# Weight forms made once for two groups, sums that read PSUM directly, and sigmoid products and projection sums at other places in the queues

## The chip, the cores and the metric

The kernel runs on one core of a Trainium2 chip. The metric is the device time of one execution in microseconds (us); of several executions the median is given. TensorE (PE) multiplies matrices and writes into PSUM, its weight load (PEld) overlaps its matmuls; VectorE (DVE), ScalarE (ACT) and GpSimd (POOL) do element-wise work, SyncE (SP) issues transfers. Each engine works off its own queue in order, and waits on semaphores for the others.

## The reference, cut to what matters

```python
# r, k, v: (4, 8, 768, 48); w, u: (8, 48)
for t in range(S):
    cur = einsum('bhd,bhe->bhde', u[None] * kt, vt)
    y[:, :, t] = einsum('bhd,bhde->bhe', rt, state + cur)
    state = w[None, :, :, None] * state + einsum('bhd,bhe->bhde', kt, vt)
x = y.transpose(0, 2, 1, 3).reshape(3072, 384)
g = x @ w_gate                       # (384, 1536)
silu = g * (1.0 / (1.0 + exp(-g)))
val = x @ w_val                      # (384, 1536)
out = silu * val @ w_out             # (1536, 384)
```

A linear attention with decay runs over 768 positions, and its output passes through a gated feed-forward block. All of it is fp32. This change concerns the feed-forward block alone.

## The kernel before, in words

The 3072 tokens are cut into 24 blocks of 128 (6 chunks of positions by 4 batches), and two blocks make a group, so there are 12 groups. The attention is computed block by block in a loop over s; between its steps, pieces of the feed-forward block that are ready are taken from a list `todo` (`feed`, `gaps`). Everything is issued in an order that the Python code writes out: `manual_schedule` keeps each engine's queue in that order, and the framework adds semaphores and gives tiles their buffers.

Groups 0 and 1 compute gate and value by plain products (`gate_value`, L445). Groups 2 to 7 go in pairs through `four_units` (L638): 7 products and 4 more in place of 12 for each block of 128 columns of the weights. Groups 8 to 11 go in two pairs, called group 8 and group 10 here, through `three_units` (L788). It takes three blocks of 128 columns (f = 3t to 3t+2) by three blocks of the 384 inputs by the two groups of tokens, and makes the result of 18 block products from 15 (`ROUNDS`, L672). A unit t (0 to 3) has 15 steps; each step (`three_step`, L774) multiplies a weight form by a token form, for gate and for value (o = 0, 1). Seven chains of steps accumulate in PSUM banks: n, y, l4, l5, l1, l2 and l8, of which n, y, l5, l1 and l8 share four buffers of pool ps_a.

- `in_place(t)` (L689) turns three of the nine weight blocks of unit t into forms where they lie in `wgv`, with six operations on GpSimd. It is called in `prepare_threes` (L760) at projection items 0, 2, 4 and 6 of groups 6 and 7, after `four_units` is through with these weights.
- `w_forms(g, t)` (L701) makes the six other forms r2, r3, r13, r11, r5 and r9, with nine operations on GpSimd (L720), in a ring buffer or in `spare`, a list of tiles that the attention no longer needs. It is done once for group 8 and once more for group 10: for group 8 and t = 0 at projection item 7, for group 10 and t = 0, 1 at items 2 and 6 of group 8's projections, for the others during unit t - 1, one operation behind each of its steps.
- `x_forms(g)` (L730) makes eleven sums of token blocks on VectorE (L744 to L754).
- `later(at, do, out, ...)` (L800) puts an operation behind step `at` of the unit, in the queue of its engine; z = 15 t. A name in quotes is a PSUM bank. ScalarE copies banks into SBUF tiles (q10, q14, r12, r6, x, y), VectorE adds up the six results c[0] to c[5], and GpSimd adds y to r6 (L827).
- `silu` (L803) issues a sigmoid on ScalarE (L806) and two products (L807, L808) on the engine `on`, behind step `muls`. For c[4], c[5] these are on GpSimd; for the other results of units 0 to 2 they are on VectorE, both pairs behind step 7 of the next unit; in unit 3 one pair is on VectorE and one on GpSimd.
- `two_projections(g)` (L652) multiplies the hidden values by w_out in seven products per group in place of eight (`project`, L499), in the order of 14 items "00 10 01 02 11 04 03 12 05 06 13 14 15 16" (first digit: which of the two groups). Their input sums come from `h_sums` (L487, operations at L493, L494, L496 and L497), in a ring buffer hs of pool `three`, tag w_bits, with three buffers.

At the end (L1033 to L1042) the list `tail` puts the units of group 8, its projections, the units of group 10 (whose first two steps stand among the last projections) and its projections in one order.

```python
later(z + 10.4, dve.tensor_add, c[2], y, "l1")
later(z + 10.5, dve.tensor_add, c[5], q10, "l5")
later(z + 11.5, dve.tensor_add, r12, r12, "l2")
later(z + 12.5, dve.tensor_add, c[3], r6, "l8")
```

Step 13 adds to bank l1 again, step 14 to l2; so step 13 waits until c[2] has been read from l1, and step 14 until r12 has read l2 (in unit 3 these two steps change places).

Of the kernel before, what the change touches and what calls it, by code (L numbers as in the profile page):

```python
# [9 lines left out]
FP32 = mybir.dt.float32  # L10
# [12 lines left out]
def fast(  # L23
# [47 lines left out]
    wcol = cst.tile([P, HP], FP32, name="wcol")  # L71
    ub = cst.tile([P, H, D], FP32, name="ub")
    kscale = cst.tile([P, H, D], FP32, name="kscale")
    rscale = cst.tile([P, H, D], FP32, name="rscale")
    w128 = cst.tile([P, HP], FP32, name="w128")
# [150 lines left out]
    def own_product(i):  # L226
        kl, rl = raw(i)
        rk = two.tile([P, H, D], FP32, name="rk", tag="rk")[:]
        pool.tensor_mul(rk, rl, kl)
        pool.tensor_mul(rk, rk, ub[:])  # L230
        rks[i] = rk
# [16 lines left out]
    sp.dma_start(  # L248
        out=ub[:].rearrange("p h d -> p (h d)"),
        in_=bass.AP(tensor=u.tensor, offset=u.offset, ap=[[0, P], [1, H * D]]),  # L250
# [50 lines left out]
    def scale_k(i):  # L301
        pool.tensor_mul(khat[i % 4][:, :, 0:D], raw(i)[0], kscale[:])

    def scale_r(i):
        pool.tensor_mul(rhat_of(i)[:, :, 0:D], raw(i)[1], rscale[:])  # L305

    def natural_tables():
        for t, dst in ((pw[:, :, 1 : P + 1], kscale), (pv, rscale)):
            t_ps = ps_a.tile([P, HP, P], FP32, name="t_ps", tag="a")
            for a in range(HP):  # L310
                pe.transpose(t_ps[:, a, :], t[:, a, :], ident[:])
            act.copy(dst[:], t_ps[:].rearrange("p a (e x) -> p (a e) x", e=2)[:, :, 0:D])

# [173 lines left out]
    def h_sums(g, n):  # L487
        h11, h12, h21, h22 = h_quarters(g)
        t = three.tile([P, 2, FH, P], FP32, name="hs", tag="w_bits")
        x = part_of.setdefault(g, {})  # L490
        x["s"] = x.get("s", ()) + (t[:, 0], t[:, 1])
        if n == 0:
            dve.tensor_add(t[:, 0], h22, h21)  # L493
            dve.tensor_sub(t[:, 1], t[:, 0], h11)  # L494
# [143 lines left out]
    def four_units(g):  # L638

        steps = sorted((11 * f - 5 + at, f, what) for f in range(FC) for what, at in PLACE.items())  # L640
        pieces = [[] for _ in range(26)]
        n = 0
        for at, f, what in steps:
            k = max(n - 1, 0) if n < 4 else 3 + min(23 * (n - 4) // (11 * FC - 4), 22)
            if what == "p1" and f % 2 == 0 and f + 2 < FC:
                pieces[k].append(lambda f=f: w_sums(g, f + 2))
            k = (0, 1, 2, 2)[n] if n < 4 else k
            pieces[k].append(lambda f=f, what=what: four(g, f, what))
            n += what[0] in "pc"
        return [lambda q=q: [do() for do in q] for q in pieces]  # L650

    def two_projections(g):  # L652

        def item(j, p):
            if (j, p) in ((1, 0), (0, 1)):
                h_sums(g, p)
# [29 lines left out]
    spare += [t[:].rearrange("p a x -> p (a x)")[:, 0:256] for t in v_ld + Z]  # L686
    wide = {}

# [11 lines left out]

    def w_forms(g, t):  # L701

        f = 3 * t
        made = wide["u", g, t] = {}

        w = [[wgv[:, :, c, P * (f + i) : P * (f + i + 1)] for c in range(CC)] for i in range(3)]
        def place():
            if g > THREES and t < 2:
                s = [x.rearrange("p (o t) -> p o t", o=2) for x in spare[6 * t : 6 * t + 6]]
            else:  # L710
                ring = three.tile([P, 6, 2, P], FP32, name="s", tag="w_bits")
                s = [ring[:, n] for n in range(6)]
            made.update(zip(("r2", "r3", "r13", "r11", "r5", "r9"), s))
            made.update({
                "r0": w[1][1], "r1": w[0][1], "r4": w[0][0], "r6": w[1][2], "r7": w[2][2],
                "r8": w[1][0], "r10": w[2][0], "r12": w[0][2], "r14": w[2][1],
            })

        return [place] + [
            lambda o=o, a=a, b=b, op=op: op(made[o], made[a], made[b])  # L720
            for o, a, b, op in (
                ("r2", "r14", "r6", pool.tensor_sub), ("r3", "r8", "r1", pool.tensor_sub),
# [37 lines left out]
    def prepare_threes(g, n):  # L760
        if g == THREES:
            if n in (0, 2, 4, 6):
                in_place(n // 2)
            if n == 7:
                for do in w_forms(g, 0):
                    do()
        else:
            if n == 10:
                x_forms(g)
            if n in (2, 6):  # L770
                for do in w_forms(g, n // 4):
                    do()

    def three_step(g, t, n):  # L774
# [6 lines left out]
        u, v = wide["u", g, t][what], wide["v", g][what]  # L781
        for o in range(2):
# [5 lines left out]
    def three_units(g):  # L788
# [14 lines left out]
        def silu(at, n, which, h, on, muls):  # L803
# [4 lines left out]
            todo.append((muls + 0.1, lambda: on.tensor_mul(h, sg, value)))  # L808

        for t in range(4):  # L810
            z = 15 * t
            for n in range(15):
                todo.append((z + n, lambda t=t, n=n: three_step(g, t, n)))
            if ("u", g, t + 1) not in wide and t < 3:
                forms = w_forms(g, t + 1)
                todo.append((z + 0.1, forms[0]))
                todo += [(z + n + 0.2, do) for n, do in enumerate(forms[1:])]
            later(z + 0.5, act.copy, q10, "n")
# [6 lines left out]
            later(z + 8.5, act.copy, x, "n")  # L825
            later(z + 9.5, act.copy, y, "y")
            later(z + 9.6, pool.tensor_add, r6, y, r6)  # L827
            later(z + 10.4, dve.tensor_add, c[2], y, "l1")
            later(z + 10.5, dve.tensor_add, c[5], q10, "l5")
            later(z + 11.5, dve.tensor_add, r12, r12, "l2")  # L830
# [14 lines left out]
        pieces = []  # L845
# [188 lines left out]
    projections = two_projections(THREES), two_projections(THREES + 2)  # L1034
    for t in range(2):
        wide["u", THREES + 2, t] = None
    threes = three_units(THREES), three_units(THREES + 2)
# [418 lines left out]
```

## Time and profile before

| what | before |
| --- | --- |
| median of 3 runs | 629.29 us (628.3 to 630.57) |
| the profiled execution | 627.92 us, of it 626.2 us from the first to the last instruction (the span) |
| TensorE clock granted | 0.997 |
| TensorE busy | 604.1 us |
| VectorE / GpSimd / ScalarE busy | 404.1 / 374.3 / 234.7 us |
| units of group 8 | 449.4 to 506.4 us |
| projections of group 8 | 506.4 to 537.6 us |
| units of group 10, from step 2 | 537.6 to 591.3 us |
| projections of group 10, output | 591.3 to 626.2 us |

All times within the execution are us from its first instruction. A line of the timeline gives start, duration, engine, line of the code, operation, output and inputs with their shapes, how many instructions follow each other, and in brackets how long the engine had been idle before it, and for which instruction it waited. In the table of waits a line gives who waited for whom, the total in us, how many times, and the longest one.

### The profile page before, as it was taken

How to read it: one execution, taken by the hardware profiler on the slowest of the kernel's cores; microseconds unless marked ns; L12 is line 12 of the kernel's file. 1: busy time of each engine (PE TensorE's matmuls, PEld its weight loads, DVE VectorE, ACT ScalarE, POOL GpSimd, SP SyncE). 2: the span in 40 equal slices, each digit the busy share in tenths (PEclk: the TensorE clock that was granted, in tenths of full speed). 3: DMA queues.
4: the chain of work that ended last, by engine and by line, in shares of the span. 5: the costliest groups of instructions: out<-in, count | busy, mean ns of one | idle time of the engine just before them, and what ended most of it. 6: DMA issues, size and time to landing. Idle time of an engine off the chain costs nothing.

```text
span 626.2 us, 12872 instructions
## 1 busy us (share of the span) xinstructions
PE 604.1 (96%) x4992; PEld 541.6 (86%) x4992; DVE 404.1 (65%) x737; ACT 234.7 (37%) x599; POOL 374.3 (60%) x414
## 2 busy tenths in 40 slices
PE   8799999999999999999999999999999989999986
PEld 7688888899888899888899888899887779977886
DVE  6878997373556573466575466666457896588770
ACT  3368785312444412344331334532233320233310
POOL 4789789935566315475453647389857459178210
PEclk9999999999999999999999999999999999999998
DMA  7989873234232113323222311230100000000001
GB/s 178 228 213 250 258 240 65 49 63 85 55 59 35 38 18 72 69 40 55 37 40 62 76 20 29 33 49 17 39 1 2 1 1 26 26 0 1 1 2 54
DMA packets 138006, 40.45 MB, mean 65 GB/s; under 512 B 128592, under 2 KB 131792, under 8 KB 137936
## 3 DMA queue, kind: packets, MB, share of 16 engines
q1 hardware_dynamic: 134480, 34.82, 26.2%
q10 hardware_dynamic: 3456, 4.72, 2.1%
q8 instruction: 41, 0.67, 0.5%
q14 instruction: 29, 0.24, 0.1%
HBM read 28.51 MB, written 4.72 MB: 53 GB/s over the span
## 4 chain that ended last, share of the span: by engine, by line
PE 76%; DVE 10%; POOL 4%; issue 1%; SPq 1%; DMA 1%; ACT 1%; DVEq 0%; ACTq 0%; POOLq 0%
PE c_b L620 13%; PE o_f L520 12%; PE c_a L620 11%; PE o_a L520 7%; PE gv L449 7%; PE c_l L783 6%; PE o_b L520 6%; PE y_ps L412 5%; PE s_ps L382 3%; DVE hats L801 3%; PE c_n L783 2%; DVE hTs L808 2%; PE c_y L783 2%; DVE At L807 2%; SPq L359 1%
## 5 line engine op out<-in xcount | busy, mean ns | idle before, releaser
L449 PE MATMUL gv<-xT,wgv 128*128 128x256 f32 x288 | 66.8, 385 | 0.6 <-ACT xT L416 0.6
L323 ACT ACTIVATE At<-ident,du 128x128 f32<-128x128 f32 x176 | 61.0, 396 | 16.2 <-DVE du L235 7.3
L620 PE MATMUL c_b<-xT,wgv 128*128 128x256 f32 x216 | 64.5, 380 | 0.0
L604 POOL TENSOR_TENSOR hTs<-hTs,u 128x256 f32<-128x256 f32 x36 | 28.7, 799 | 56.4 <-DVE hTs L603 56.2
L449 PEld LDWEIGHTS gv<-xT,wgv 128*128 128x128 f32 x288 | 53.2, 190 | 8.9 <-ACT xT L416 0.9
L620 PEld LDWEIGHTS c_b<-xT,wgv 128*128 128x128 f32 x216 | 40.7, 190 | 5.3
L387 DVE COPY_PREDICATED At<-mask,s_ps 128x512 f32<-128x512 int32 x48 | 33.0, 743 | 18.0 <-PE s_ps L382 9.4
L627 ACT COPY u<-c_a 128x256 f32<-128x256 f32 x72 | 26.7, 371 | 47.0 <-PE c_a L620 46.0
L620 PE MATMUL c_a<-t,s 128*128 128x256 f32 x144 | 43.5, 383 | 0.4 <-ACT p L627 0.4
L620 PE MATMUL c_a<-xT,wgv 128*128 128x256 f32 x144 | 42.8, 379 | 0.0
L305 POOL TENSOR_TENSOR hats<-r_ld,rscale 128x384 f32<-128x384 f32 x20 | 21.1, 1057 | 33.8 <-DMA hats<-hats 33.8
L600 ACT ACTIVATE sg<-hTs 128x256 f32<-128x256 f32 x72 | 29.9, 416 | 30.2 <-DVE hTs L629 21.3
L620 PE MATMUL c_b<-xT,s 128*128 128x256 f32 x144 | 37.0, 379 | 0.0
L634 DVE TENSOR_TENSOR u<-u,c_b 128x256 f32<-128x256 f32 x36 | 15.0, 417 | 33.0 <-PE c_b L620 30.1
L412 PE MATMUL y_ps<-At,v_ld 128*32 128x128 f32 x768 | 34.9, 273 | 1.4 <-DVE At L387 1.4
L801 POOL TENSOR_TENSOR kT<-y,kT 128x512 f32<-128x512 f32 x8 | 11.5, 1440 | 38.0 <-ACT y L801 38.0
L412 PEld LDWEIGHTS y_ps<-At,v_ld 128*32 128x32 f32 x768 | 30.3, 110 | 2.4 <-issue 1.4
L582 POOL TENSOR_TENSOR s<-wgv 128x256 f32<-128x256 f32 x18 | 13.3, 738 | 30.6 <-PE o_f L520 28.8
L440 POOL TENSOR_TENSOR Z<-Z,w 48x192 f32<-48x192 f32 x32 | 18.1, 567 | 21.7 <-DVE Z L439 20.5
L620 PEld LDWEIGHTS c_a<-t,s 128*128 128x128 f32 x144 | 26.8, 190 | 4.4 <-ACT p L627 0.8
L620 PEld LDWEIGHTS c_b<-xT,s 128*128 128x128 f32 x144 | 27.2, 190 | 3.9
L620 PEld LDWEIGHTS c_a<-xT,wgv 128*128 128x128 f32 x144 | 27.3, 190 | 3.6
(217 smaller groups left out, 1600.0 us busy)
## 6 DMA issues: line engine op xcount, KB each, us to landing
hats<-hats SPq DMA_DIRECT2D x192, 32.0 KB, 2.0
w_bits<-in_moe_w_gate_dram SPq DMA_DIRECT2D x6, 768.0 KB, 5.9
v_ld<-in_v_dram SPq DMA_DIRECT2D x48, 96.0 KB, 3.3
w_bits<-in_moe_w_val_dram SPq DMA_DIRECT2D x6, 768.0 KB, 6.3
w_bits<-in_moe_w_out_dram SPq DMA_DIRECT2D x6, 768.0 KB, 6.5
out_dram<-o_sb ACTq DMA_DIRECT2D x24, 192.0 KB, 2.0
k_ld<-in_k_dram SPq DMA_DIRECT2D x20, 192.0 KB, 3.0
r_ld<-in_r_dram SPq DMA_DIRECT2D x20, 192.0 KB, 3.8
```

The source lines that it names most:

```text
L305: pool.tensor_mul(rhat_of(i)[:, :, 0:D], raw(i)[1], rscale[:])
L323: lambda h=h: act.activation(At[i % 2][:, h, :], ident[:], AF.Identity, scale=du[:, h : h + 1])
L387: dve.copy_predicated(At[i % 2][:].rearrange("p (a e) t -> p a e t", e=2)[:, :, e], mask[:].bitcast(INT32).unsqueeze(1).to_broadcast([P, H ...
L412: pe.matmul(ps[32 * q : 32 * q + 32, cc, :], *x, start=start, stop=stop, skip_group_check=True,)
L449: pe.matmul(gv[:, o, :].rearrange("p (i t) -> p i t", i=2), wt[:, c, P * f : P * (f + 1)], xT[:, 2 * g % NX : 2 * g % NX + 2, c, :], start ...
L520: pe.matmul(ps, lhs[:, f, :], rhs[:, f, :], start=(f == 0 and n in (0, 1, 4)), stop=(f == FH - 1), skip_group_check=True,)
L600: act.activation(x[what, f][:], h[j], AF.Sigmoid)
L604: pool.tensor_mul(h[1], h[1], x.pop(("u3", f))[:])
L620: pe.matmul(ps.rearrange("p (i t) -> p i t", i=2), lhs, rhs, start=first, stop=what not in ("p2", "p5", "p4", "p3"), skip_group_check=True,)
L627: act.copy(x[nm, f][:], ps)
L783: pe.matmul(wide[chain][:, o].rearrange("p (i t) -> p i t", i=2), u[:, o], v, start=first and o == 0, stop=True, skip_group_check=True,)
L801: todo.append((at, lambda: do(out, *(bank(a) if isinstance(a, str) else a for a in args))))
```

## The change

- `w_forms` no longer takes the group: the forms are made once, for group 8, and group 10 uses the same. Unit 0 has its forms in the ring buffer; those of units 1 to 3 lie in tiles that are free by then: the three scale tables, now one tile `scales`, two token slots of `xT`, and `spare`.
- `in_place(0)` to `in_place(2)` are called in `four_units(6)`, behind the products h1 of f = 2, 5 and 8; `in_place(3)` at projection item 1. The forms of unit 1 and then of unit 0 follow, two operations per item; those of units 2 and 3 stand in group 8's units, one per 2.1 steps.
- r6 is summed by VectorE out of bank y, ahead of ScalarE's copy of y. c[0] is taken from bank n itself, not from the copy x, and directly behind r12. c[5] goes ahead of c[2]; in unit 3, c[2] goes behind r12.
- Of the two silu pairs of units 0 to 2 on VectorE, one is moved from behind step 7 to behind step 2 of the next unit. In unit 3 the second pair is on VectorE in place of GpSimd, and is issued at projection item 01.
- Input sums of the projections of groups 8 to 11 lie in two ring buffers for even groups and in the tile of c for odd ones.

In the built program the copy of y waits for VectorE's sum r6, which reads the same bank, and bank l8 takes the buffer of y, where it took that of n.

```diff
@@ four_units
+            if g + 2 == THREES and what == "h1" and f % 3 == 2 and f < 11:
+                pieces[k].append(lambda f=f: in_place(f // 3))
@@ two_projections, item
+            if g >= THREES and (j, p) == (0, 1):
+                for do in wide.pop("last"):
+                    do()
@@ h_sums
-        t = three.tile([P, 2, FH, P], FP32, name="hs", tag="w_bits")
+        if g < THREES:
+            t = three.tile([P, 2, FH, P], FP32, name="hs", tag="w_bits")
+        else:
+            t = room["hs"][2 * (g % 2) + n]
@@ w_forms
-    def w_forms(g, t):
+    def w_forms(t):
...
-            if g > THREES and t < 2:
-                s = [x.rearrange("p (o t) -> p o t", o=2) for x in spare[6 * t : 6 * t + 6]]
-            else:
+            if t == 0:
                 ring = three.tile([P, 6, 2, P], FP32, name="s", tag="w_bits")
                 s = [ring[:, n] for n in range(6)]
+            else:
+                s = (early + spare)[6 * t - 6 : 6 * t]
+                s = [x.rearrange("p (o t) -> p o t", o=2) for x in s]
@@ prepare_threes
-        if g == THREES:
-            if n in (0, 2, 4, 6):
-                in_place(n // 2)
-            if n == 7:
-                for do in w_forms(g, 0):
-                    do()
-        else:
+        if g > THREES:
             if n == 10:
                 x_forms(g)
-            if n in (2, 6):
-                for do in w_forms(g, n // 4):
-                    do()
+            return
+        if n == 1:
+            in_place(3)
+            todo_forms.extend(w_forms(1))
+        if n == 7:
+            todo_forms.extend(w_forms(0))
+        for _ in range(2):
+            if todo_forms:
+                todo_forms.popleft()()
@@ three_units
+        if g == THREES:
+            forms = w_forms(2) + w_forms(3)
+            todo += [(2.1 * n + 0.2, do) for n, do in enumerate(forms)]
         for t in range(4):
...
-            if ("u", g, t + 1) not in wide and t < 3:
-                forms = w_forms(g, t + 1)
-                todo.append((z + 0.1, forms[0]))
-                todo += [(z + n + 0.2, do) for n, do in enumerate(forms[1:])]
...
-            later(z + 9.5, act.copy, y, "y")
-            later(z + 9.6, pool.tensor_add, r6, y, r6)
-            later(z + 10.4, dve.tensor_add, c[2], y, "l1")
-            later(z + 10.5, dve.tensor_add, c[5], q10, "l5")
+            later(z + 9.5, dve.tensor_add, r6, "y", r6)
+            later(z + 9.6, act.copy, y, "y")
+            later(z + 10.4, dve.tensor_add, c[5], q10, "l5")
+            later(z + (11.55 if t == 3 else 10.5), dve.tensor_add, c[2], y, "l1")
...
-            later(z + r0 + 0.1, dve.tensor_sub, c[0], r12, x)
+            later(z + 11.6, dve.tensor_sub, c[0], r12, "n")
...
-                    silu(at, 1 - n, room["c"][:, 0:2, n], hTs[:, n, 9:11], (dve, pool)[n], at + 0.1)
+                    silu(at, 1 - n, room["c"][:, 0:2, n], hTs[:, n, 9:11], dve, (at + 0.1, 1e9)[n])
                 else:
                     silu(z + 15.8 + n, 1 - n, room["c"][:, 1 - n], hTs[:, :, 3 * t + 1 - n],
-                         dve, z + 22.3 + n / 4)
+                         dve, z + (17.3, 22.3)[n])
...
+            if at >= 1e9:
+                last.append(do)
+                continue
...
+        pieces[-1].append(lambda: wide.update(last=last))
@@ end of fast
+    room["hs"] = [
+        three.tile([P, 2, FH, P], FP32, name="hs", tag="w_bits")[:] for _ in range(2)
+    ] + [room["c"][:].rearrange("p i j o t -> p (i j o t)")[:, 1536 * n : 1536 * n + 1536]
+         .rearrange("p (s f t) -> p s f t", s=2, f=FH) for n in range(2)]
```

More of the change, by code (lines that the diff above doesn't have):

```diff
@@ L71, in fast @@
     wcol = cst.tile([P, HP], FP32, name="wcol")
-    ub = cst.tile([P, H, D], FP32, name="ub")
-    kscale = cst.tile([P, H, D], FP32, name="kscale")
-    rscale = cst.tile([P, H, D], FP32, name="rscale")
+    scales = cst.tile([P, 3, H, D], FP32, name="scales")
+    ub, kscale, rscale = (scales[:, n] for n in range(3))
     w128 = cst.tile([P, HP], FP32, name="w128")
@@ L229, in own_product @@
         pool.tensor_mul(rk, rl, kl)
-        pool.tensor_mul(rk, rk, ub[:])
+        pool.tensor_mul(rk, rk, ub)
         rks[i] = rk
@@ L248, in fast @@
     sp.dma_start(
-        out=ub[:].rearrange("p h d -> p (h d)"),
+        out=ub.rearrange("p h d -> p (h d)"),
         in_=bass.AP(tensor=u.tensor, offset=u.offset, ap=[[0, P], [1, H * D]]),
@@ L301, in scale_k @@
     def scale_k(i):
-        pool.tensor_mul(khat[i % 4][:, :, 0:D], raw(i)[0], kscale[:])
+        pool.tensor_mul(khat[i % 4][:, :, 0:D], raw(i)[0], kscale)
     def scale_r(i):
-        pool.tensor_mul(rhat_of(i)[:, :, 0:D], raw(i)[1], rscale[:])
+        pool.tensor_mul(rhat_of(i)[:, :, 0:D], raw(i)[1], rscale)
     def natural_tables():
@@ L311, in natural_tables @@
                 pe.transpose(t_ps[:, a, :], t[:, a, :], ident[:])
-            act.copy(dst[:], t_ps[:].rearrange("p a (e x) -> p (a e) x", e=2)[:, :, 0:D])
+            act.copy(dst, t_ps[:].rearrange("p a (e x) -> p (a e) x", e=2)[:, :, 0:D])
     def scale(i):
@@ L686, in fast @@
     spare += [t[:].rearrange("p a x -> p (a x)")[:, 0:256] for t in v_ld + Z]
-    wide = {}
+    flat = scales[:].rearrange("p n h d -> p (n h d)")
+    early = [flat[:, 256 * n : 256 * n + 256] for n in range(4)]
+    flat = xT[:, 4:6].rearrange("p i c t -> p (i c t)")
+    early += [flat[:, 256 * n : 256 * n + 256] for n in range(2)]
+    wide, todo_forms = {}, deque()
     def in_place(t):
@@ L699, in in_place @@
             pool.tensor_sub(o, o, b)
-    def w_forms(g, t):
+    def w_forms(t):
         f = 3 * t
-        made = wide["u", g, t] = {}
+        made = wide["u", t] = {}
         w = [[wgv[:, :, c, P * (f + i) : P * (f + i + 1)] for c in range(CC)] for i in range(3)]
         def place():
-            if g > THREES and t < 2:
-                s = [x.rearrange("p (o t) -> p o t", o=2) for x in spare[6 * t : 6 * t + 6]]
-            else:
+            if t == 0:
                 ring = three.tile([P, 6, 2, P], FP32, name="s", tag="w_bits")
                 s = [ring[:, n] for n in range(6)]
+            else:
+                s = (early + spare)[6 * t - 6 : 6 * t]
+                s = [x.rearrange("p (o t) -> p o t", o=2) for x in s]
             made.update(zip(("r2", "r3", "r13", "r11", "r5", "r9"), s))
@@ L717, in place, with form @@
             })
+        def form(o, a, b, op):
+            op(made[o], made[a], made[b])
         return [place] + [
-            lambda o=o, a=a, b=b, op=op: op(made[o], made[a], made[b])
-            for o, a, b, op in (
+            lambda x=x: form(*x) for x in (
                 ("r2", "r14", "r6", pool.tensor_sub), ("r3", "r8", "r1", pool.tensor_sub),
@@ L780, in three_step @@
             wide[chain] = pool_of.tile([P, 2, 2 * P], FP32, name=f"c_{chain}", tag=tag)
-        u, v = wide["u", g, t][what], wide["v", g][what]
+        u, v = wide["u", t][what], wide["v", g][what]
         for o in range(2):
@@ L840, in three_units @@
                     at = z + 13.7 + n
-                    silu(at, 1 - n, room["c"][:, 0:2, n], hTs[:, n, 9:11], (dve, pool)[n], at + 0.1)
+                    silu(at, 1 - n, room["c"][:, 0:2, n], hTs[:, n, 9:11], dve, (at + 0.1, 1e9)[n])
                 else:
                     silu(z + 15.8 + n, 1 - n, room["c"][:, 1 - n], hTs[:, :, 3 * t + 1 - n],
-                         dve, z + 22.3 + n / 4)
-        pieces = []
+                         dve, z + (17.3, 22.3)[n])
+        pieces, last = [], []
         for at, do in sorted(todo, key=lambda x: x[0]):
+            if at >= 1e9:
+                last.append(do)
+                continue
             if at == int(at):
@@ L1034, in fast @@
     projections = two_projections(THREES), two_projections(THREES + 2)
-    for t in range(2):
-        wide["u", THREES + 2, t] = None
+    room["hs"] = [
+        three.tile([P, 2, FH, P], FP32, name="hs", tag="w_bits")[:] for _ in range(2)
+    ] + [room["c"][:].rearrange("p i j o t -> p (i j o t)")[:, 1536 * n : 1536 * n + 1536]
+         .rearrange("p (s f t) -> p s f t", s=2, f=FH) for n in range(2)]
     threes = three_units(THREES), three_units(THREES + 2)
```

## The prediction

> **What bounds the kernel now.** I read the busy shares first, then the table of who waits for whom restricted to TensorE, then the timeline of the last 180 us, which is the part that the change touches.
>
> ```profile
> PE 604.1 (96%) x4992; PEld 541.6 (86%) x4992; DVE 404.1 (65%) x737; ACT 234.7 (37%) x599; POOL 374.3 (60%) x414
> ```
>
> TensorE is busy for 604.1 of 626.2 us. No matmul is added or removed, so the change can only win idle time of TensorE, or add some. The waits of TensorE from 449 us to the end (total us, times, longest):
>
> ```profile
> PE o_a L520 <- DVE hs L494: 3.7, 2, 1.9
> PE c_l L783 <- DVE hats L801: 3.7, 4, 1.1
> PE c_l L783 <- DVE xf L750: 0.7, 1, 0.7
> PE c_l L783 <- DVE kT L801: 0.4, 2, 0.2
> PE c_l L783 <- DVE xf L747: 0.4, 1, 0.4
> ```
>
> Every one of them is a wait for VectorE. From 300 to 450 us the same table has one wait, 0.4 us, for ScalarE. The timeline (start, us, engine, line) shows how VectorE comes to be late: in unit t=2 of the first group,
>
> ```profile
> 487.30 1.21 DVE L807 TENSOR_TENSOR At<-At,hats 128x512 f32<-128x512 f32 x1
> 487.84 1.89 PE L783 MATMUL c_l<-k_ld,wgv 128*128 128x256 f32 x8
> 487.92 1.74 POOL L801 TENSOR_TENSOR kT<-y,kT 128x512 f32<-128x512 f32 x1
> 488.54 1.67 DVE L808 TENSOR_TENSOR hTs<-At,hats 128x512 f32<-128x512 f32 x1
> 490.13 0.67 DVE L801 TENSOR_TENSOR hats<-y,c_l 128x512 f32<-128x512 f32 x1
> 490.86 1.13 PE L783 MATMUL c_l<-xf,wgv 128*128 128x256 f32 x4 [1.13 <-DVE hats L801]
> 492.06 1.13 PE L783 MATMUL c_l<-r_ld,wgv 128*128 128x256 f32 x4
> 493.02 1.03 PE L783 MATMUL c_n<-xf,wgv 128*128 128x256 f32 x4
> ```
>
> and in the projections behind that group
>
> ```profile
> 508.40 4.06 PE L520 MATMUL o_f<-wo,hTs 128*128 128x192 f32 x24
> 511.23 0.95 DVE L493 TENSOR_TENSOR hs<-hTs 128x768 f32<-128x768 f32 x1
> 512.11 1.26 POOL L807 TENSOR_TENSOR At<-At,hats 128x512 f32<-128x512 f32 x1 [4.78 <-ACT At L806]
> 512.21 1.98 DVE L494 TENSOR_TENSOR hs<-hs,hTs 128x768 f32<-128x768 f32 x1
> 514.33 2.19 PE L520 MATMUL o_a<-wt,hs 128*128 128x192 f32 x12 [1.86 <-DVE hs L494]
> ```
>
> The four sigmoid products of a unit stand in one run in VectorE's queue (L807, L808, twice) and last 0.98 to 1.67 us each while GpSimd works, against 0.68 when it is silent (500.04, 501.37). The sum that frees bank l1 stands behind them.
>
> **The size of what can be won.** A step of 15-product work (two halves) takes 0.865 us undisturbed (459.78 to 460.65), a unit 12.97; a projection product 1.95. Distance between two starts less the steps between them is lost time:
>
> - start of group 8: 449.43 to 454.60, four steps: 5.17 - 3.46 = 1.71
> - t=1: 473.60 to 478.35: 1.29; t=2: 487.84 to 493.02: 1.72; t=3: 502.52 to 506.45: 0.47
> - its projections: 508.40 to 514.33 less 3.90: 2.03; before o_b at 535.80: 0.16
> - group 10: t=1 1.35 (558.36 to 563.17), t=2 1.74, t=3 0.48, projections 2.04 (593.25 to 599.19)
>
> Sum 13.0 us. More than that the change cannot win.
>
> [...] L808 takes 1.67 beside GpSimd and 0.69 alone, while the sums that read a PSUM bank take 0.67 to 0.69 in both cases. [...] the trace has 1.29 to 1.74 us for r6 on GpSimd against 0.68 on VectorE from PSUM. [...]
>
> **The change, part by part.** Times in a unit are from its first step U; a result can be read 1.06 to 1.13 us after its step starts (458.06 to 459.12).
>
> *Forms once.* 36 of 72 form operations (0.72 to 1.4 us each on GpSimd) go, all in group 10 or the projections before it. GpSimd is not TensorE's releaser, so their own time is worth nothing; what they free is VectorE. In group 8 the 18 forms of t=2 and 3 remain, spread at one per 2.1 steps in place of nine per unit.
>
> *In-place sums earlier.* 18 operations (4.4 us per block of six at 0.73) move between the h1 products at about 371, 385 and 412 us. Behind the second stand chunk 22's scale_r (ended 387.6) and own product (389.7): 4.4 us later is 392.0 and 394.1, against move_blocks at 396.09 on the SP queue and the sum du at 397.61. Both hide; no DMA moves. w_sums for f=10 ends near 397.7, some 10 us before TensorE's use. The third stands where block 0 stood before. Cost nothing; contended at 1.44 per operation the second would be 8.6 us and du 0.7 late, still 20 us ahead of its scores at 420.37.
>
> *Start of group 8.* GpSimd then has 24 operations from 420.4 where it had 36 up to 452.3. The ring buffer of forms(0) comes free when projection o_f ends at 437.1, nine forms of 0.73 make 443.7, and the next form needs At1, read until about 449.4. So the first four x_forms, from 448.13, run at 0.34 us pitch and not 0.9; L747 ends at 449.6 where TensorE wants it at 451.2. From 449.5 five forms do overlap: 449.5 + 3 x 0.85 puts L750 at 452.05 against 451.8. Of 1.71 some 0.3 stays.
>
> *Products split.* The first pair now stands at step 2.3, where VectorE is idle from 1.6 to 4.5; contended (2.7) it ends at 5.0, and the sums behind catch up by 6.3. The second stands at 6.95 and ends at 8.3 if GpSimd is silent. In group 10 it is; in group 8 the forms that follow the first silu are done about U+5.5.
>
> *Sums from PSUM.* r6 moves from GpSimd to VectorE: from U+8.91 to 9.60. c[5] 9.71 to 10.39, c[2] 10.31 to 10.99, r12 to 11.59, c[0] (now reading bank n, uncontended where kT,x took 0.88 to 1.48) to 12.19. The weight load of step 13 wants l1 at 11.03, that of step 14 wants l2 at 11.89: free. So t=1 and t=2 lose 0.1 (group 8) and 0.05 (group 10).
>
> *The added wait.* The y copy on ScalarE now waits for r6 (same bank): 9.64 to 10.22. And l8 (step 12) now takes y's bank, not n's: its weight load, due at 10.16, is let go at about 10.27. On TensorE everything stands behind it. Bound per unit: 0 (a stalled load gives back 0.1, as 492.06 to 493.02 shows: 0.96, not 1.075) to 0.12; I take 0.06, 0.5 for eight units. If r6 is late by d, all is late by d.
>
> *t=3 and the projections.* r12 goes ahead of c[2]: done at 11.25 against 11.03, 0.2 stays of 0.47. c[0] leaves the stretch ahead of the silu (0.6 us), and the other silu's products leave GpSimd for after the first h sums, so L494 takes 0.95, not 1.98. h sums end at U+19.0; TensorE wants them at 18.84 to 18.95: 0.1 stays of 2.03. The deferred products (1.4) end at 20.4, o_b wants them at 20.9. The odd group's input sums now lie in c (tile hats), which group 10 writes first at step 6; the last projection that reads them stands before step 2, so that hides.
>
> Remaining: 0.3 + 2 x 0.1 + 2 x 0.05 + 2 x 0.2 + 2 x 0.1 + 0.5 = 1.7. Won: 13.0 - 1.7 = 11.3 us. The profiled execution (span 626.2, 627.92 in all; what lies around the span is untouched) would become 616.6. The median shown is 1.37 above it, so 629.29 - 11.3 = 618.0.
>
> **Rivals.**
>
> *A, half given back.* The forms left in group 8 run into both pairs of products and into x_forms, and the y chain is late by 0.2 to 0.3 per unit. Lost again: 1.4 (start), 1.4 (half of t=1 and t=2 in group 8), 8 x 0.25 = 2.0. Won 6.5, time 622.8; between this and the forecast if only some of it holds. For it: three deadlines lie within 0.2 us of their sums. Against: in group 10 nothing contends.
>
> *B, slower: r6 on VectorE becomes the pace.* Place: y copy and with it l8 in all eight units. It decides if r6 ends more than 11.3 / 8 = 1.4 us late, beyond U+11.0; at 1.9 late the time is 629.3 + 8 x 0.5 = 633. VectorE would have to be busy until 10.8, the second pair taking 3.9 us; the longest pair seen is 1.22 + 1.67 = 2.89, beside GpSimd. Per unit VectorE has 12 x 0.61 + 4 x 0.7 = 10.1 us of work, 12.97 of time.
>
> *C, no change.* VectorE is late for another cause and the waits only move a step on: 629. Against it: VectorE idles 2.3 us ahead of the q14 sum in every unit (2.30 at 497.61), so its queue, not its load, makes it late.
>
> **How the numbers follow.** Forecast 0.72, A 0.20, C 0.05, B 0.03. Low: all 13.0 won, 616.3, less 0.5 for scatter of the median (runs of before span 2.3 us): 615.8. High: 621.8, which takes in the forecast and more than half of the way to A. Within 0.3% (1.9 us) is about what a measurement cannot tell from no change: same 0.03, slower 0.03, faster 0.94.
>
> **What would show it.** Right: TensorE's waits for hats and for hs fall under 0.3 us each; units of 13.0 to 13.3 us; L494 at 0.95; the second L808 of a unit near 0.7 in group 10; x_forms' first four under 0.5. Wrong: a wait of TensorE on ScalarE's y copy above 0.2 us per unit, L808 still at 1.67 before r6, or a new wait on scores or w_sums before 449 us.

## The result and the profile after

The changed kernel takes 622.01 us (median of 4 runs, 621.22 to 622.28), the kernel before 628.81 us beside it (628.30 to 630.57): a ratio of 0.9885, 95% interval 0.9862 to 0.9907. That is 6.8 us won, where 11.3 were forecast and 618.0 us expected; the time lies 0.2 us above the range. The profiled execution took 621.22 us, its span is 619.5 us against 626.2.

Lines of the code have moved: the products L807 and L808 are now L821 and L822, the sums of `later` L815, the input sums L758 to L768, the matmuls of the 15-product work L797, of the four-product work L622, of the projections L522, the h1 product L606, the in-place sums L709 and L710.

The busy shares of the page after the change:

```profile
PE 601.7 (97%) x4992; PEld 541.5 (87%) x4992; DVE 396.8 (64%) x749; ACT 234.7 (38%) x599; POOL 324.7 (52%) x366
```

GpSimd has 48 operations and 50 us less to do. TensorE's waits from the start of group 8 (453 us) to the end were five rows and 8.9 us before; this is the whole table now (total us, times, longest):

```profile
PE c_l L797 <- DVE xf L764: 1.1, 1, 1.1
```

The wait for `hats` and the wait for `hs` are gone. The timeline of unit t=2 in group 8 shows why (VectorE's rows, and TensorE's row of step 13):

```profile
487.88 0.69 DVE L821 TENSOR_TENSOR At<-At,hats 128x512 f32<-128x512 f32 x1
488.60 0.69 DVE L822 TENSOR_TENSOR hTs<-At,hats 128x512 f32<-128x512 f32 x1
489.76 0.69 DVE L815 TENSOR_TENSOR kT<-c_y,kT 128x512 f32<-128x512 f32 x1 [0.47 <-PE c_y L797]
...
491.16 0.68 DVE L815 TENSOR_TENSOR hats<-y,c_l 128x512 f32<-128x512 f32 x1
491.76 0.68 DVE L815 TENSOR_TENSOR kT<-kT,c_l 128x512 f32<-128x512 f32 x1
492.10 1.03 PE L797 MATMUL c_l<-xf,wgv 128*128 128x256 f32 x4
```

Only one pair of products stands ahead of r6 (489.76), VectorE even idles 0.47 us before it, and the sum that frees l1 (491.16) is ready before TensorE's step 13 at 492.10, which has no wait in brackets. In the projections behind that group

```profile
508.91 4.06 PE L522 MATMUL o_f<-wo,hTs 128*128 128x192 f32 x24
510.82 0.95 DVE L495 TENSOR_TENSOR hs<-hTs 128x768 f32<-128x768 f32 x1
511.80 0.96 DVE L496 TENSOR_TENSOR hs<-hs,hTs 128x768 f32<-128x768 f32 x1
512.68 0.69 DVE L821 TENSOR_TENSOR At<-At,hats 128x512 f32<-128x512 f32 x1
512.91 2.19 PE L522 MATMUL o_a<-wt,hs 128*128 128x192 f32 x12
```

L496 takes 0.96 us in place of 1.98, and o_a starts 4.00 us behind o_f, 0.10 late in place of 2.03.

So the part that the prediction spoke of did what it should: from the first step of group 8 to the end of the span it took 176.8 us before (449.43 to 626.2) and takes 166.0 now (453.49 to 619.5), 10.8 us less. But group 8 starts 4.06 us later than before. That loss lies in front of all the waits that the prediction listed. TensorE's waits from 300 to 453 us:

```profile
PE c_a L622 <- ACT p L629: 2.6, 2, 2.2
```

One of the two, 0.4 us, was there before. Setting each matmul beside its counterpart in the trace before gives the places of the loss: 0.58 us in the first 30 us, 0.65 at 189 us, 2.5 at 398 us, 0.3 at 416 us.

The 2.5 us come from GpSimd's queue. Call the f-th block of 128 columns of the weights tile f; its h1 product, on GpSimd, finishes its hidden values. GpSimd's timeline from tile 5's h1 product to tile 6's (rows left out are more of the six in-place sums, the two scalings, the two own products and the five w sums):

```profile
386.20 0.73 POOL L606 TENSOR_TENSOR hTs<-hTs,u 128x256 f32<-128x256 f32 x1 [3.22 <-DVE hTs L605]
386.88 0.73 POOL L709 TENSOR_TENSOR wgv<-wgv 128x256 f32<-128x256 f32 x1
...
390.87 0.79 POOL L710 TENSOR_TENSOR wgv<-wgv 128x256 f32<-128x256 f32 x1
391.62 1.01 POOL L301 TENSOR_TENSOR hats<-k_ld,scales 128x384 f32<-128x384 f32 x1
...
394.63 1.00 POOL L229 TENSOR_TENSOR rk<-rk,scales 128x384 f32<-128x384 f32 x1
395.60 0.72 POOL L584 TENSOR_TENSOR s<-wgv 128x256 f32<-128x256 f32 x1
...
398.76 0.90 POOL L588 TENSOR_TENSOR s<-wgv 128x256 f32<-128x256 f32 x1
399.62 0.72 POOL L606 TENSOR_TENSOR hTs<-hTs,u 128x256 f32<-128x256 f32 x1
```

and of ScalarE and TensorE:

```profile
400.37 0.37 ACT L629 COPY p<-c_a 128x256 f32<-128x256 f32 x1 [3.58 <-POOL hTs L606]
400.80 0.70 PE L622 MATMUL c_a<-t,s 128*128 128x256 f32 x2 [2.24 <-ACT p L629]
```

Read from the end: TensorE adds to bank c_a again only after ScalarE has copied p out of it. ScalarE had been idle for 3.58 us before this copy, and waited for GpSimd's L606, tile 6's h1 product. The copy writes a buffer of the pool `six` (tag part, six buffers), and in the program as built its buffer comes free with the h1 product that reads u3 of three tiles before. That product stands behind in-place sums, scalings, own products and w sums, and starts 13.4 us after tile 5's. Before the change the same two rows were

```profile
393.52 0.73 POOL L604 TENSOR_TENSOR hTs<-hTs,u 128x256 f32<-128x256 f32 x1
396.13 0.37 ACT L627 COPY p<-c_a 128x256 f32<-128x256 f32 x1 [0.57 <-PE c_a L620]
```

The product ended at 394.25, the copy began at 396.13: 1.88 us of room. The block put 4.9 us in front of it (6.10 later on the clock of the profile, of which 1.23 is lost earlier).

### The profile page after: what moved, and what is told of

It reads as the page before. It is cut to its first block, busy times and chain, and to the rows that moved or that the text cites. A ratio compares the mean times of both kernels' runs of the same rounds, so it can differ in the third digit from the quotient of the medians.

```text
span 619.5 us, 12800 instructions
## 1 busy us (share of the span) xinstructions
PE 601.7 (97%) x4992; PEld 541.5 (87%) x4992; DVE 396.8 (64%) x749; ACT 234.7 (38%) x599; POOL 324.7 (52%) x366
## 4 chain that ended last, share of the span: by engine, by line
PE 78%; POOL 7%; SPq 3%; DVE 3%; DMA 2%; issue 1%; ACT 1%; DVEq 0%; POOLq 0%; ACTq 0%
PE o_f L522 13%; PE c_b L622 10%; PE c_l L797 10%; PE c_a L622 9%; PE o_a L522 8%; PE gv L448 7%; PE o_b L522 6%; PE y_ps L411 4%; PE c_y L797 3%; PE c_n L797 3%; SPq L358 3%; PE s_ps L381 3%; POOL wgv L216 1%; DMA hats<-hats 1%; POOL hTs L606 1%
## 5 line engine op out<-in xcount | busy, mean ns | idle before, releaser
L622 PE MATMUL c_b<-xT,wgv 128*128 128x256 f32 x216 | 64.5, 380 | 0.0
L821 POOL TENSOR_TENSOR At<-At,hats 128x512 f32<-128x512 f32 x8 | 10.2, 1272 | 97.9 <-ACT At L820 97.9
L606 POOL TENSOR_TENSOR hTs<-hTs,u 128x256 f32<-128x256 f32 x36 | 27.9, 774 | 51.3 <-DVE hTs L605 51.0
L622 PE MATMUL c_a<-t,s 128*128 128x256 f32 x144 | 43.7, 385 | 2.9 <-ACT p L629 2.9
L622 PEld LDWEIGHTS c_b<-xT,wgv 128*128 128x128 f32 x216 | 40.8, 190 | 5.3
L622 PE MATMUL c_a<-xT,wgv 128*128 128x256 f32 x144 | 42.9, 379 | 0.0
L304 POOL TENSOR_TENSOR hats<-r_ld,scales 128x384 f32<-128x384 f32 x20 | 21.0, 1049 | 32.0 <-DMA hats<-hats 32.0
L622 PE MATMUL c_b<-xT,s 128*128 128x256 f32 x144 | 37.0, 379 | 0.0
L622 PEld LDWEIGHTS c_a<-t,s 128*128 128x128 f32 x144 | 26.6, 190 | 7.6 <-ACT p L629 4.1
L631 DVE TENSOR_TENSOR hTs<-p,c_b 128x256 f32<-128x256 f32 x36 | 15.0, 417 | 24.8 <-PE c_b L622 22.3
L622 PEld LDWEIGHTS c_b<-xT,s 128*128 128x128 f32 x144 | 27.2, 190 | 3.9
L622 PEld LDWEIGHTS c_a<-xT,wgv 128*128 128x128 f32 x144 | 27.3, 190 | 3.5
L411 PE MATMUL y_ps<-rT,Z 112*32 112x128 f32 x480 | 29.8, 276 | 0.3 <-ACT kT L347 0.3
```

Source lines behind the costliest of these rows:

```text
L304: pool.tensor_mul(rhat_of(i)[:, :, 0:D], raw(i)[1], rscale)
L411: pe.matmul(ps[32 * q : 32 * q + 32, cc, :], *x, start=start, stop=stop, skip_group_check=True,)
L606: pool.tensor_mul(h[1], h[1], x.pop(("u3", f))[:])
L622: pe.matmul(ps.rearrange("p (i t) -> p i t", i=2), lhs, rhs, start=first, stop=what not in ("p2", "p5", "p4", "p3"), skip_group_check=True,)
```

## The experiments

Theory R (ring): the second block of in-place sums delays a product on GpSimd that frees a buffer, and TensorE waits at the end of that chain. Its rivals: the loss is scatter of the start, or contention, or plain overload of GpSimd. Every ratio is to runs of the kernel before made beside it on the same chip; "tail" is the time from the first step of group 8 to the start of the last row of matmuls, read in the one profiled execution of each kernel (before 169.3 us, the changed kernel 158.49).

**The block moved on, and the block moved alone.**

```diff
-            if g + 2 == THREES and what == "h1" and f % 3 == 2 and f < 11:
-                pieces[k].append(lambda f=f: in_place(f // 3))
+            if g + 2 == THREES and what == "h1" and f in (2, 7, 8):
+                pieces[k].append(lambda f=f: in_place((2, 7, 8).index(f)))
```

> The changed kernel, with the second block of six in-place sums put behind the h1 product of tile 7 instead of tile 5; nothing else. Theory R (ring): in the changed kernel the block, the two scalings, the two own products and five w sums stand ahead of tile 6's h1 product on GpSimd (386.9 to 399.6 us); that product frees a buffer of the six-buffer ring of product parts, ScalarE's copy of p waits for it and TensorE 2.24 us for the copy. Behind tile 7 the block has GpSimd's idle time from 402 us on: the 2.24 us wait goes, time 622.0 - 2.2 = 619.8. Theory S (start): the time lost ahead of 449 us comes from the first 190 us and differs from run to run: no change, 622. Theory C (contention): the block slows VectorE's sums wherever it stands in the four-product work: no change or worse, 622 to 623.

Measured: 617.12 us (616.92 to 617.59), ratio 0.9824, interval 0.9808 to 0.9840. All matmuls up to group 8 stand within 0.2 us of the kernel before, and of the waits from 300 to 453 us the old one alone is left:

```profile
PE c_a L622 <- ACT p L629: 0.4, 1, 0.4
```

That is 2.7 us less than theory R expected: it priced the wait alone, and the unaltered changed kernel, run again below, shows what else hangs on it.

The other way round, the kernel before with the blocks moved as the change moves them:

```diff
+            if g + 2 == THREES and what == "h1" and f % 3 == 2 and f < 11:
+                pieces[k].append(lambda f=f: in_place(f // 3))
...
-            if n in (0, 2, 4, 6):
-                in_place(n // 2)
+            if n == 6:
+                in_place(3)
```

> The kernel before, with the three blocks of in-place sums moved into the four-product work of group 6 as the change does; nothing else of the change. Theory R: a TensorE wait of about 2.2 us for ScalarE's copy of p at about 398 us and 0.3 at 412; against it the start of group 8 loses less (GpSimd less in arrears there), at most 0.4 of its 1.71 us: about 629 + 2.5 - 0.4 = 631. Theory S: no change, 629, or up to 0.5 faster.

Measured: 630.96 us, ratio 1.0040, interval 1.0027 to 1.0053. The wait of 2.24 us is there, at 399.59; group 8's start loses 1.0 us less than before (behind by 2.86 us at its second step, by 1.88 at its fourth). So moving the blocks, without the rest of the change, makes the kernel before slower, and with the second block behind tile 7 the change wins 10.9 us. Theory R holds in both directions; the theory of contention is out.

**Only the product taken off GpSimd.**

```diff
-            pool.tensor_mul(h[1], h[1], x.pop(("u3", f))[:])
+            on = dve if (g, f) == (6, 6) else pool
+            on.tensor_mul(h[1], h[1], x.pop(("u3", f))[:])
```

> The changed kernel, with one h1 product (that of tile 6, the one that frees the ring buffer) on VectorE instead of GpSimd; the second block of in-place sums stays behind tile 5. Theory R (ring): the buffer comes free as soon as VectorE has it (some 0.42 us more there), however long GpSimd's queue is: the 2.24 us wait at 398 us goes, and with it the stretch of half clock that follows it in some executions: 617.1 to 618. Theory O (GpSimd is simply overloaded around 390 us, and the wait moves to the next thing that it is late with: tile 7's product, the block move, the w sums of tiles 10 and 11): a wait of 1 us or more stands later in the same unit, 620 or more.

Measured: 617.10 us (616.71 to 618.33), ratio 0.9820, interval 0.9806 to 0.9833; from 380 to 420 us TensorE waits for nothing. GpSimd does the block where the change put it, with one operation less behind it. What cost time was the one product that frees the buffer, not GpSimd's load.

**The block made longer.**

```diff
             op(o, o, a)
             pool.tensor_sub(o, o, b)
+            if t == 1:
+                pool.tensor_copy(o, o)
+                pool.tensor_copy(o, o)
```

> The changed kernel, with six copies of a weight block onto itself on GpSimd inside the second block of in-place sums (the values stay the same), so this block is longer by 6 d, d being what such a copy takes (the nearest row, a sum of the same shape, has 0.73 us). Theory R: GpSimd's queue is the whole chain up to the ring buffer, so TensorE's wait for ScalarE's copy of p grows one for one, to 2.24 + 6 d (up to 6.6 us). Theory K (clock): the stretch of half TensorE clock that followed the wait of 2.24 us in four of seven profiled executions (1.8 us lost each) follows the wait; after a longer one it is there in the profiled execution, and the five times lie closer together than the 2.3 us of the changed kernel. Sum: 619.9 + 6 d + 1.8. If the half clock has another cause, it is there or not as before.

Measured: 625.02 us (623.32 to 626.49), ratio 0.9950, interval 0.9930 to 0.9969. A copy takes 0.40 us and the block is 2.84 us longer (7.58 from its first sum to the scaling behind it, against 4.74). The wait grew by 2.92, one for one; TensorE's timeline has

```profile
403.05 1.16 PE L622 MATMUL c_a<-t,s 128*128 128x256 f32 x2 [5.16 <-ACT p L629]
```

The granted clock is 0.50 from 404 to 406 us; the next run has the same. The second half of theory K missed: the six times do not lie closer together, they span 3.2 us.

**The changed kernel once more**, unaltered.

> The changed kernel once more, unaltered. Its profiled execution stood 1.23 us behind the kernel before ahead of the second block of in-place sums (0.58 from the first 30 us, 0.65 at 189 us), where the program does the same work. If that is the start's own scatter (waits for the first loads), it is another number here, below 0.5 in most executions, and the time comes out at about 621; the 2.24 and 0.3 us at 398 and 412 us return. If it belongs to the changed kernel (other places of its tables), it returns, and so does 622.

Measured: 620.98 us (619.73 to 622.02), ratio 0.9876, interval 0.9858 to 0.9895. The first 397 us now agree with the kernel before within 0.2 us, so the 1.23 us of the first profile (0.58 in the first 30 us, 0.65 at 189 us) are scatter between executions. The 2.24 us return, and with them something new. TensorE's rows after the wait, in this execution:

```profile
399.47 0.70 PE L622 MATMUL c_a<-t,s 128*128 128x256 f32 x2 [2.23 <-ACT p L629]
400.01 0.59 PE L622 MATMUL c_b<-xT,wgv 128*128 128x256 f32 x2
400.44 1.49 PE L622 MATMUL c_b<-xT,s 128*128 128x256 f32 x4
401.72 1.06 PE L622 MATMUL c_a<-t,s 128*128 128x256 f32 x2
```

and its windows (stretch, length, PE busy, granted clock, DMA share, GB/s):

```profile
400.00:401.00 1.00, 1.00 (x6) 0.93 0.42 54
401.00:402.00 1.00, 1.00 (x4) 0.50 0.36 48
402.00:403.00 1.00, 1.00 (x3) 0.50 0.34 50
403.00:404.00 1.00, 1.00 (x4) 0.50 0.36 59
404.00:405.00 1.00, 1.00 (x6) 0.86 0.25 39
```

Two products last 0.86 us from start to start, not 0.43: the granted clock is 0.50 from 400.87 to 404.28 in the trace's clock record, 3.41 us, and over this stretch the delay against the kernel before grows from 2.3 to 4.1 us, 1.8 us on top of the wait. Of the seven profiled executions with the 2.24 us wait four have this stretch (this one, and those with all input sums early, the sums as before, and forms twice) and three do not (the first profile, the kernel before with the blocks, the products as before). So the wait, with the 0.3 us behind it, costs 2.8 us or 4.6, by execution. The times agree: of nine runs of the changed kernel the two fastest (619.73 and 620.08) lie 2.6 and 3.0 us above the 617.12 of the version with the block behind tile 7, the others 3.9 to 5.2 (one of these is the first profile, with its 1.23 us of scatter).

**Each part of the change undone.** The two sums as before:

```diff
-            later(z + 9.5, dve.tensor_add, r6, "y", r6)
-            later(z + 9.6, act.copy, y, "y")
-            later(z + 10.4, dve.tensor_add, c[5], q10, "l5")
-            later(z + (11.55 if t == 3 else 10.5), dve.tensor_add, c[2], y, "l1")
+            later(z + 9.5, act.copy, y, "y")
+            later(z + 9.6, pool.tensor_add, r6, y, r6)
+            later(z + 10.4, dve.tensor_add, c[2], y, "l1")
+            later(z + 10.5, dve.tensor_add, c[5], q10, "l5")
...
-            later(z + 11.6, dve.tensor_sub, c[0], r12, "n")
+            later(z + r0 + 0.1, dve.tensor_sub, c[0], r12, x)
```

> The changed kernel, with the two sums as before: y copied by ScalarE first, r6 summed from the copy on GpSimd; output 0 from the copy of x at the end of the unit and not from bank n; the sum that frees l1 ahead of c5 again. Products stay split, forms are made once. Theory Q (the order of VectorE's queue is what made it late, and the products are its core): t=0 to 2 lose nothing more, since GpSimd's r6 stands beside sums that read PSUM; in t=3 the c[0] sum ahead of the sigmoid costs 0.6 to 0.9 us in the chain to the h sums, and l1 0.3: 622.0 + 2 x 1.0 = 624.0. Theory G (taking r6 off GpSimd and its 1.3 to 1.7 us out of the chain is the core): 1 us in each of eight units, 629.

Measured: 623.31 us, ratio 0.9917 (0.9896 to 0.9938); tail 160.09, so 1.6 us. Units t=0 to 2 lose nothing, the projections about 1.0 us each time; the start of group 8, which this edit does not touch, came out 0.4 us shorter in this execution. In the table of TensorE's waits from 450 us on:

```profile
PE o_a L522 <- DVE hs L496: 1.7, 2, 0.9
```

The products as before:

```diff
-                    silu(at, 1 - n, room["c"][:, 0:2, n], hTs[:, n, 9:11], dve, (at + 0.1, 1e9)[n])
+                    silu(at, 1 - n, room["c"][:, 0:2, n], hTs[:, n, 9:11], (dve, pool)[n], at + 0.1)
...
-                         dve, z + (17.3, 22.3)[n])
+                         dve, z + 22.3 + n / 4)
```

> The changed kernel, with the sigmoid products as before: both pairs of a unit in one run on VectorE, and in t=3 the other silu's products on GpSimd right away, ahead of the input sums of the projections. Sums from PSUM and forms once stay. Theory Q: the four products stand ahead of the sum that frees l1 again. In group 10 GpSimd is silent, so they last 2.7 us and not some 4.5, and t=1, t=2 lose 0 to 0.5; in group 8 (forms beside them) 0.5 to 1.5 each; the projections lose 1.9 each again, since the GpSimd products run beside the second input sum: 622.0 + 3.8 + 2 = 627.8. Theory F (GpSimd's load is all that made VectorE late): only the projections' 3.8 come back, 625.8 or less.

Measured: 625.81 us, ratio 0.9973 (0.9961 to 0.9986); tail 164.17, so 5.7 us, the largest part. Not by the way I expected: GpSimd is silent beside all these products (0.68 to 0.69 us each, in group 8 too), and bank l1 is free in time. Four of them in a row, 2.7 us, make r6 late, and r6 is now what ScalarE's copy of y, and so bank l8, waits for, by the same 0.5 us of idle TensorE in six units; the steps behind start 0.76 us later each time. The projections lose 0.73 us each, not the 1.9 I expected: TensorE waits twice for L496, 0.7 us at the longest, with products on GpSimd beside it again (beside them this sum, then L494, took 1.98 us in the kernel before). From the same table of this kernel:

```profile
PE c_l L797 <- ACT y L815: 3.0, 6, 0.5
```

This is the wait that the prediction's rival B named, well under the 1.4 us a unit at which B turns the gain into a loss; the split of the products is what keeps it at nothing in the changed kernel.

Eighteen form operations done again in group 10 (into the same places, the same values):

```diff
         if g == THREES:
-            forms = w_forms(2) + w_forms(3)
-            todo += [(2.1 * n + 0.2, do) for n, do in enumerate(forms)]
+            forms = room["forms"] = w_forms(2) + w_forms(3)
+        else:
+            forms = room["forms"][1:10] + room["forms"][11:]
+        todo += [(2.1 * n + 0.2, do) for n, do in enumerate(forms)]
```

> The changed kernel, with the 18 form operations of t=2 and t=3 done again during group 10, at the same spacing as in group 8 and into the same places (the same values). Sums and products stay as changed. Theory Q: the split pair has room beside GpSimd too; group 8 of the changed kernel loses nothing in t=1 and t=2 with the same forms, so group 10 loses 0 to 0.3: 622.0 to 622.3. Theory F: the contention comes back to t=0 and t=1 of group 10, 1.3 us or more each: 624.5.

Measured: 620.74 us, ratio 0.9876 (0.9860 to 0.9892), no difference from the changed kernel run beside it (620.98); tail 159.32. The units of group 10 lose nothing. The 0.8 us of the tail, which the times are too scattered to show, stand in the projections of group 8, where GpSimd already makes the first of these forms and the input sum beside them takes 1.36 us, not 0.96. Its timeline there:

```profile
513.04 1.36 DVE L496 TENSOR_TENSOR hs<-hs,hTs 128x768 f32<-128x768 f32 x1
514.55 1.70 PE L522 MATMUL o_a<-wt,hs 128*128 128x192 f32 x9 [0.77 <-DVE hs L496]
```

What the three tails lose sums to 5.7 + 1.6 + 0.8 = 8.1 of 10.8 us; the other 18 form operations were not put back, and what the parts do only together was not tried apart.

**The start of group 8.** 1.44 us are left there. GpSimd's timeline in the changed kernel (first profile) has

```profile
452.76 2.52 POOL L732 TENSOR_TENSOR At<-wgv 128x256 f32<-128x256 f32 x3 [4.86 <-PE y_ps L411]
```

and VectorE's, beside these forms,

```profile
452.53 0.42 DVE L759 TENSOR_TENSOR xf<-xT 128x256 f32<-128x256 f32 x1
452.87 0.96 DVE L760 TENSOR_TENSOR xf<-xT,xf 128x256 f32<-128x256 f32 x1
...
456.47 0.83 DVE L764 TENSOR_TENSOR xf<-xf,xT 128x256 f32<-128x256 f32 x1
```

Three edits, the first on the changed kernel and the others on the version with the block behind tile 7. All eleven sums earlier:

```diff
+            if s == 24:
+                x_forms(THREES)
...
-        if s == 24:
-            x_forms(THREES)
```

> The changed kernel, with the 11 sums of group 8's input forms put ahead of the last two sums of the projections on VectorE's queue (right behind the last masked copy of scores), so some 10 us earlier; nothing else. Theory: of 4.90 us from the first to the fifth step of group 8, 1.44 is a wait for input sums that run beside the forms in At1 on GpSimd. Put ahead, they end before 452.5 even at 0.9 us each: the wait goes, 622.0 - 1.4 = 620.6. Rival: the two projection sums that then stand behind them hold the o banks, and TensorE waits for these instead: 622 or up to 1 us slower.

Measured: 620.50 us (619.71 to 622.18), ratio 0.9879 (0.9860 to 0.9898), no difference from the changed kernel run again (620.98). The rival was right. The same edit with the block behind tile 7:

> Both edits of the two other changed kernels together (second in-place block behind tile 7, group 8's input sums ahead of the last projection sums). If the two waits are separate, the gains add: 622.0 - 2.2 - 1.4 = 618.4. If removing one uncovers another stage as late, it is above 619.

Measured: 617.42 us, ratio 0.9829 (0.9813 to 0.9845), against 617.12 without it. From 430 to 470 us the wait at step 4 is gone and a longer one is there, in the last projection, for the sum that now stands behind the eleven:

```profile
PE o_b L522 <- DVE o_sb L539: 1.3, 1, 1.3
```

Four sums early and seven late (a `yield` behind the fourth splits `x_forms`):

```diff
             gaps(s, 1)
+            if s == 24:
+                early_forms = x_forms(THREES)
+                next(early_forms)
...
-            x_forms(THREES)
+            for _ in early_forms:
+                pass
```

> The changed kernel with the second in-place block behind tile 7, and the first four of group 8's input sums right behind the last masked copy of scores on VectorE, the other seven where they stood. The run with all eleven ahead traded a wait of 1.26 us at step 4 for one of 1.33 us in the last projection, whose bank VectorE's sum was late to free; four of them last 3.5 us at most and end before that sum is due (443.6 against 444.1). Expected: neither wait, 617.1 - 1.25 = 615.9. Rival: the forms in At1 run beside the seven that are left, and step 4 still waits 0.5 or more: 616.6.

Measured: 616.36 us (615.69 to 616.82), ratio 0.9811 (0.9797 to 0.9824). From 430 us to the end TensorE waits for nothing that the table lists; the tail is 157.14, 1.35 less than the changed kernel's. By the ratios the gain on the version without the split (0.9824) is within their intervals; it is the wait table and the tail that show it.

The forms out of the way instead, VectorE's queue left as it is:

```diff
-            todo += [(2.1 * n + 0.2, do) for n, do in enumerate(forms)]
+            todo += [(1.0 * n + 11.2, do) for n, do in enumerate(forms)]
```

> The changed kernel with the second in-place block behind tile 7, and the 18 forms of t=2 and t=3 issued from step 11 on at one per step, behind GpSimd's first sigmoid product, instead of from step 0 at one per 2.1 steps; nothing moved on VectorE. If contention with those forms makes the input sums of group 8 late, GpSimd is now silent beside them, they take 0.42 us each and step 4 waits for nothing: 615.9; what they cost beside the products of t=1 is below 0.3. If the place in VectorE's queue alone makes them late, step 4 waits 1.25 us as before, 617.1.

Measured: 616.03 us, ratio 0.9803 (0.9789 to 0.9816), the lowest median, not to be told from the run before. Its profiled execution took 621.16 us: near its start TensorE waited 3.5 us for a load, and its matmuls ran at half pace behind that (16 of L381 take 2.25 us at 32.32 and 1.16 at 52.35; about 10 us in all, by an estimate from such rows, at a mean granted clock of 0.991 for the execution); so only its tail is compared: 157.15. Its timeline shows that the sums are fast now:

```profile
454.22 0.42 DVE L760 TENSOR_TENSOR xf<-xT,xf 128x256 f32<-128x256 f32 x1
454.68 0.42 DVE L761 TENSOR_TENSOR xf<-xf,xT 128x256 f32<-128x256 f32 x1
454.85 1.13 PE L797 MATMUL c_n<-xf,wgv 128*128 128x256 f32 x4
```

GpSimd is silent beside them (idle for 16.81 us up to 466.08). So the forms on GpSimd made these sums late, not their place in VectorE's queue: beside the forms five of the eleven, L760 to L764, take 0.83 to 0.96 us, here each of the eleven 0.42 or 0.43.

## Why the prediction missed by 4 us

- *What bounds the kernel, and the 13.0 us of lost time:* right. TensorE stayed the bound, and its idle time was all that could be won.
- *Forms once:* right in kind. GpSimd's own time was worth nothing; what the operations give back on VectorE is 0.8 us for half of them, in the tail of one execution.
- *In-place sums earlier, "Cost nothing":* wrong, and this is the step that failed. It listed what stands behind the second block (scale_r, the own product, move_blocks, du, the w sums of f=10), found each with room, and left out the h1 product behind them, which frees a buffer of `part`. Its room before was 1.88 us, the block 4.9. Cost: 2.8 us, and 1.8 more where the clock is halved behind the wait. With the product off GpSimd, or the block behind tile 7, the change wins 11.0 or 10.9 us, of the 11.3 forecast. "a new wait on scores or w_sums before 449 us" was among the signs named; a new wait came, but on neither of the two. The first and third blocks cost nothing, as predicted (no loss at 371 or 412 us with the second out of the way); the 0.3 us at 416 us are there only in executions with the long wait.
- *Start of group 8, 0.3 stays:* 1.44 stayed. Right mechanism, size wrong: the forms in At1 were to start with group 8's first step (449.4 on the old clock), so that four input sums would run alone. GpSimd began at 452.76, 0.73 us ahead of the first step at 453.49, and two ran alone.
- *Products split, sums from PSUM:* right. The first pair takes 0.96 to 1.10 us per product beside GpSimd in group 8 and has room; units t=1 and t=2 lose nothing, where 0.1 and 0.05 were kept.
- *The added wait, 0.5 for eight units:* nothing was lost. In unit 0 the copy of y begins at 464.56 and steps 11 and 12 run as one row, at full pace. With the products in one run the wait is real, 0.5 us in six units.
- *t=3 and the projections:* 0.2 and 0.1 were kept; 0.17 and 0.19, and 0.17 twice, were measured.
- *The sum:* 1.44 + 0.17 + 0.19 + 2 x 0.17 = 2.14 us stayed, not 1.7, so 10.8 were won in the last 180 us. Less 2.8 for the second block and 1.23 for this execution's start this is 6.8; the spans differ by 6.7.
- *Rivals:* A gave nearly the measured time (622.8), but by luck: neither the pairs nor the y chain gave anything back, only the start of group 8 did, and the second block, which A does not name, made up the rest. C and B did not come.
- *Two readings of before:* the slowed products last from 0.88 us (485.36) and not 0.98, and the last row of o_b in group 8's projections starts at 535.63, not 535.80, so that about 0.05 us is lost there and not 0.16. Neither changes the forecast by more than 0.1 us.

## What to carry to other kernels

When work is put into an engine's queue, go through everything that stands behind it up to the engine's next idle time, and ask of each instruction not only who reads its result but whose buffer it frees; then read the room of that buffer in the trace, from the end of the last reader to the start of the next writer. Here it was 1.88 us, could be read from two rows, and was shorter than the block. What decided here was the place in the queue ahead of a ring's last reader, not the engine's spare time in total: the same block two products later, or that product on another engine, costs nothing.

## What the hardware showed that I had not expected

A wait of 2.24 us was followed, in four of seven executions, by a stretch of granted clock 0.50; in the one shown it lasted 3.41 us and began 1.4 us after TensorE had started again. The mean granted clock of the whole execution is 0.995 to 0.997 in the four and 0.998 to 0.999 in the three.

Two clock records show when the clock changed. The one of the kernel before has a single change, 614.399 us behind its start, the one of the changed kernel's first profile a single one, 610.986 us behind its start: 180 and 179 times 3.4133 us, called a clock step here. The stretch shown above is one clock step long, and behind the wait of 5.16 us the clock is at 0.50 for one clock step too: it was 0.57 in the mean from 403 to 404 us, 0.50 to 406 and 0.72 from 406 to 407, which puts the changes at 403.14 and 406.56. If clock steps are counted on from a change or start that the trace shows (7.43 us in the first profile, 400.87 and 403.14 in the other two), each wait has one border of a clock step inside it. This is an estimate from those figures:

| execution | wait of TensorE (us) | border inside it | longest part in one clock step | clock in the one after |
| --- | --- | --- | --- | --- |
| second block longer | 397.89 to 403.05 | 399.73 | 3.32 | 0.50 |
| changed kernel again | 397.24 to 399.47 | 397.45 | 2.02 | 0.50 |
| changed kernel, first profile | 398.56 to 400.80 | 399.96 | 1.40 | 1.00 |

In these three the slow stretch goes with where the wait falls on the clock steps, and so with how much of it falls into one. Three executions are read here and nothing was tested: no run moved the wait against the clock steps on purpose, and why the clock fell behind some of these waits and not behind others was not shown. The run with the forms moved, whose matmuls ran at half pace for about 10 us behind a wait of 3.5 us for a load, does not fit a slow stretch of one clock step.

The wait of 2.24 us, with the 0.3 us behind it, so costs 2.8 us without the slow stretch and 4.6 with it. It is not the only cause of scatter: nine runs of the changed kernel span 2.5 us (619.73 to 622.28) and the five of the version with the block behind tile 7 0.7 us (616.92 to 617.59), but the five with tile 6's product on VectorE span 1.6 us, and the kernel before, which has no such wait, 3.0 us in thirteen runs.
